# Induced attention and maxout MoE: the first part as one table of steps, its small diagonal products on GpSimd, and three high parts of the main loop made on VectorE

## The chip, the cores and the metric

One core of a Trainium2 chip runs one program. The metric is device microseconds of one execution, as the median of several. The kernel before takes 813.03 us.

## What is computed

```python
def mab(q, kv):                       # scale = 1/sqrt(128)
    a = softmax(scale * (q @ kv.transpose(0, 2, 1)))
    return a @ kv
h = mab(I, x)                         # I: 32 inducing rows, x: 4 x 12544 x 128
a = mab(x, h).reshape(50176, 128)
out = maximum(maximum(a @ w1, a @ w2), a @ w3) @ w_out      # 128 -> 768 -> 128
```

All data is float32. The kernel writes a float32 number as a high part of fewer bits (`hi`, cast to the type fp32r) and a low part (`lows`, the number less its high part) and multiplies the parts, so that TensorE's fast fp32r products keep the precision.

## The kernel before

The work has two stages. In the first stage the 12544 tokens of a batch lie in 7 groups, group 0 of 2 tiles and groups 1 to 6 of 16 tiles (of 128 tokens). For each group TensorE makes scores against the inducing rows (`attend_products`, line 353), VectorE takes the maximum (`mq`, line 391), a product with a small diagonal matrix `md` (line 398 makes it on ScalarE, line 405 multiplies) spreads the maxima over the partitions, VectorE reduces them (`mneg`, line 410), ScalarE takes the exponential (line 436), VectorE transposes (`aT`, line 465), and TensorE adds up the weighted tokens (line 489). The 7 partial results are combined to `hT` (line 663).

Batches 1 to 3 also come transposed from memory. Batch 0 doesn't: TensorE transposes its tiles (line 343), four to a bank, and ScalarE copies them out (line 345). So batch 0's first stage has nothing to hide behind and runs at the start of the program. Beside it the four weights come in as words of 64 bits and are converted on VectorE, in six steps each: `t` and `T` (lines 240, 244), `pw` (249), `rest` (253), an addition of `rest` and `t` (261, on GpSimd for three of the weights) and `dst` (265). `wcat` (269) is made of w1 and w3 less w2 on GpSimd, two instructions of 128x768.

The second stage has chunks of 512 tokens (the first chunk, of batch 0's group 0, has 256) and for each chunk 6 slots, one for each 128 of the 768 columns. A slot is a call of `advance` (line 813): TensorE makes `pu` and `pv` (820, 826), ScalarE a Relu of `pu` (835), VectorE their maximum `h` (853), ScalarE the high part `hi` (842), GpSimd, or VectorE for some of the slots, `lows` (850, 856). Six slots later TensorE multiplies both by `wo_hi` and `wo_lo` (lines 884 to 887). `h` needs a bank of which there are two, so TensorE waits for VectorE when `h` is late by more than one slot. 600 slots of this make up nearly all of the time, and the first part of the next batch runs inside them.

The scheduler is off: each engine works in the order in which the code issues its instructions. `phase1_first` (line 545) does batch 0's first stage in a loop over groups with the lists `LOADS` (the order of the DMA loads on SyncE's queue) and `WORK` (which steps of the weights stand behind which group), and the string `ORDER` sets the steps between `hT` and the main loop. Four buffers hold the 16-tile groups, and one more the sixth, so group 6's load waits until group 2 is used up.

## Time and profile before

| | |
|---|---|
| median of 3 runs (lowest, highest) | 813.03 us (812.34, 813.15) |
| span of the profiled execution | 811.8 us (its own time is not given apart; the median is 1.2 us above the span) |
| granted TensorE clock, mean | 1.000 |
| TensorE busy | 800.6 us (99%) |
| ScalarE busy | 734.8 us (91%) |
| GpSimd busy | 648.2 us (80%) |
| VectorE busy | 628.0 us (77%) |

The busy times are sums over the instructions of an engine. TensorE's part is 99% because 600 slots keep it filled; the eight-tenths of the first slice of the profile's forty are where it isn't.

### The profile page before, as it was taken

The page shows a single profiled execution, that of the slowest core. Times are in us where ns is not written, and L with a number is a line of the kernel's source. Part 1 is how long each engine was busy: PE and PEld are TensorE (multiplying, and loading weights), DVE is VectorE, ACT ScalarE, POOL GpSimd, SP SyncE. Part 2 cuts the span into 40 slices and gives each one's busy share as a digit, 9 for nine tenths or more (in the row PEclk, how much of TensorE's full clock was granted, in tenths as well). Part 3 has the DMA queues.
Part 4 walks back from the last instruction along what each step waited for, and adds up shares of the span by engine and source line. Part 5 has one row for each costly group of instructions (what it writes and reads, how often), then busy time and mean ns, then how long its engine had stood idle before and what let it go on. Part 6 is the DMA issues. An engine that isn't in the chain of part 4 may idle for free.

```text
span 811.8 us, 14334 instructions
## 1 busy us (share of the span) xinstructions
PE 800.6 (99%) x4561; PEld 629.4 (78%) x4561; DVE 628.0 (77%) x1067; ACT 734.8 (91%) x1532; POOL 648.2 (80%) x520
## 2 busy tenths in 40 slices
PE   8989999999999999999999999999999999999998
PEld 5758778777777787787877877878878788787887
DVE  4878878777877887877886878778778778778874
ACT  6779889899998998988998989889989999899996
POOL 1269879788788887886987978878879889788887
PEclk9999999999999999999999999999999999999999
DMA  8843234274542633533734426334223222222221
GB/s 327 318 141 111 75 122 145 85 244 157 178 134 69 192 116 103 192 117 108 233 113 123 118 99 197 112 105 134 69 77 102 66 72 78 66 87 73 62 79 52
DMA packets 52842, 102.51 MB, mean 126 GB/s; under 512 B 18208, under 2 KB 22176, under 8 KB 47520
## 3 DMA queue, kind: packets, MB, share of 16 engines
q1 hardware_dynamic: 52624, 101.47, 39.6%
q8 instruction: 36, 0.59, 0.3%
q14 instruction: 38, 0.31, 0.1%
q10 hardware_dynamic: 144, 0.13, 0.0%
HBM read 48.12 MB, written 25.69 MB: 91 GB/s over the span
## 4 chain that ended last, share of the span: by engine, by line
PE 96%; DMA 2%; SPq 1%; issue 0%; ACT 0%; DVE 0%; POOL 0%; POOLq 0%; ACTq 0%; DVEq 0%
PE acc L885 17%; PE pu L820 17%; PE pv L826 17%; PE acc L886 16%; PE acc L887 16%; PE aux L734 3%; PE acc L884 3%; PE acc L489 3%; PE aux L353 2%; DMA xg<-in_x_dram 2%; PE pu L343 0%; SPq L169 0%; PE pv L343 0%; POOL us L693 0%; PE aux L700 0%
## 5 line engine op out<-in xcount | busy, mean ns | idle before, releaser
L850 POOL TENSOR_TENSOR lows<-h,hi 128x512 fp32r<-128x512 f32 (+1 forms) x504 | 633.5, 1291 | 122.1 <-ACT hi L842 121.4
L853 DVE TENSOR_TENSOR h<-pv,ru 128x512 f32<-128x512 f32 (+1 forms) x600 | 403.4, 674 | 159.1 <-PE pv L826 99.8
L835 ACT ACTIVATE ru<-pu 128x512 f32<-128x512 f32 (+1 forms) x600 | 387.3, 645 | 51.3 <-PE pu L820 49.0
L842 ACT CAST hi<-h 128x512 fp32r<-128x512 f32 (+1 forms) x600 | 398.6, 664 | 0.3 <-DVE h L853 0.3
L820 PE MATMUL pu<-pT,us 128*128 128x512 f32 (+1 forms) x600 | 231.8, 387 | 1.8 <-ACT hi L842 0.9
L885 PE MATMUL acc<-hi,wo_hi 128*128 128x512 f32 (+1 forms) x594 | 231.8, 390 | 0.0
L826 PE MATMUL pv<-pT,us 128*128 128x512 f32 (+1 forms) x600 | 231.8, 386 | 0.1
L886 PE MATMUL acc<-hi,wo_lo 128*128 128x512 f32 (+1 forms) x594 | 228.9, 385 | 0.0
L887 PE MATMUL acc<-lows,wo_hi 128*128 128x512 f32 (+1 forms) x594 | 228.8, 385 | 0.0
L885 PEld LDWEIGHTS acc<-hi,wo_hi 128*128 128x128 f32 x594 | 111.5, 188 | 29.3 <-issue 7.5
L820 PEld LDWEIGHTS pu<-pT,us 128*128 128x128 f32 x600 | 112.5, 188 | 26.8 <-ACT ru L835 1.5
L826 PEld LDWEIGHTS pv<-pT,us 128*128 128x128 f32 x600 | 112.6, 188 | 23.7 <-DVE h L853 1.2
L887 PEld LDWEIGHTS acc<-lows,wo_hi 128*128 128x128 f32 x594 | 111.5, 188 | 22.7
L886 PEld LDWEIGHTS acc<-hi,wo_lo 128*128 128x128 f32 x594 | 111.6, 188 | 21.7
L856 DVE TENSOR_TENSOR lows<-h,hi 128x512 fp32r<-128x512 f32 x96 | 76.5, 797 | 0.8 <-ACT hi L842 0.8
L898 ACT COPY o<-acc 128x512 f32<-128x512 f32 (+1 forms) x96 | 61.6, 641 | 0.0
L884 PE MATMUL acc<-pT,us 128*128 128x512 f32 (+1 forms) x99 | 38.1, 385 | 0.0
L489 PEld LDWEIGHTS acc<-xg,aT 128*32 128x32 f32 x672 | 18.7, 110 | 9.4 <-issue 5.8
L353 PE MATMUL aux<-xT,iT 128*32 128x512 f32 x184 | 24.2, 597 | 1.7 <-ACT xT L345 1.7
L734 PE MATMUL aux<-xT,hT 128*32 128x512 f32 x192 | 25.1, 603 | 0.0
L261 POOL TENSOR_TENSOR rest<-rest,t 128x768 f32<-128x768 f32 x3 | 5.5, 1819 | 24.4 <-DVE rest L253 24.4
L489 PE MATMUL acc<-xg,aT 128*32 128x128 f32 x672 | 22.5, 273 | 0.0
(151 smaller groups left out, 446.2 us busy)
## 6 DMA issues: line engine op xcount, KB each, us to landing
out_dram<-o SPq DMA_DIRECT2D x95, 256.0 KB, 2.2
xg<-in_x_dram SPq DMA_DIRECT2D x23, 1024.0 KB, 5.9
xT<-in_xt_dram SPq DMA_DIRECT2D x18, 1024.0 KB, 5.3
pT<-ph SPq DMA_DIRECT2D x192, 64.0 KB, 2.0
pT<-pl SPq DMA_DIRECT2D x192, 64.0 KB, 2.0
raw<-in_w_dram SPq DMA_DIRECT2D x3, 768.0 KB, 8.5
us<-uh SPq DMA_DIRECT2D x24, 52.0 KB, 1.9
us<-ul SPq DMA_DIRECT2D x24, 52.0 KB, 2.6
```

The source lines that it names most:

```text
L489: nc.tensor.matmul(out=hps[q * M : (q + 1) * M, :], lhsT=aT[g][:, t * M : (t + 1) * M], rhs=xgs[g][:, t, :], start=(first[q] == k), stop=( ...
L820: nc.tensor.matmul(out=pu[:, :w], lhsT=state[c.b]["us"][:, 2 * j * P : (2 * j + 1) * P], rhs=c.pT[:, :w], start=True, stop=True)
L826: nc.tensor.matmul(out=pv[:, : d.w], lhsT=state[d.b]["us"][:, (2 * j + 1) * P : (2 * j + 2) * P], rhs=d.pT[:, : d.w], start=True, stop=True,)
L835: nc.scalar.activation(out=ru[:, :w], in_=pu[:, :w], func=AF.Relu)
L842: nc.scalar.copy(out=hi[:, : c.w], in_=h[:, : c.w])
L850: nc.gpsimd.tensor_sub(**args)
L853: nc.vector.tensor_max(out=h[:, : d.w], in0=pv[:, : d.w], in1=relus.pop(s)[:, : d.w])
L856: nc.vector.tensor_sub(**low)
L884: nc.tensor.matmul(out=to, lhsT=us[:, 2 * DF :], rhs=c.pT[:, cs], start=True, stop=False)
L885: nc.tensor.matmul(out=to, lhsT=wo_hi[:, j, :], rhs=c.hh[j][:, cs], start=False, stop=False)
L886: nc.tensor.matmul(out=to, lhsT=wo_lo[:, j, :], rhs=c.hh[j][:, cs], start=False, stop=False)
L887: nc.tensor.matmul(out=to, lhsT=wo_hi[:, j, :], rhs=c.hl[j][:, cs], start=False, stop=(j == NJ - 1))
```

## The change

The loop over groups is gone. One string has a step of one to five characters for each piece of work up to the main loop, and a function looks each up: `l` a load, `T` transposes and `C` the copy out of them (these were one call before), `S`, `M`, `D`, `P`, `L`, `E`, `V`, `U`, `K` the steps of a group, `w` with a number and a letter the steps of a weight (0 is w2, 1 w_out, 2 w1, 3 w3). The order on all engines is new. Beside it:

- `md` is made on GpSimd, for each of the 7 groups, and no longer on ScalarE.
- Group 6 has a buffer of its own, so its load waits for nobody.
- The low part of w_out (`wo_lo`) and the high part are steps of their own; `wo_lo` now follows the first `lows` on GpSimd.
- The high parts of the main slots 0, 6 and 8 are cast on VectorE.

```diff
-    LOADS = (0, 1, 2, 7, 3, 8, 4, 5, 9, 6, 10)
-    WORK = (
...
-    ORDER = "a a a a b a a b 0 c e m b a b a f b a p b 1 c s b b b s S m b q 2 c s 3 c s g s s s"
+    FIRST = (
+        "k0 l1 l0 k1 x1 T1.4 C1.4 x0 T1.8 li T0.0 is C0.0 l2 T1.12 C1.12 S0 l7 C1.8 T1.0 l3 M0 x2 next D0 "
...
+    )
...
+        elif (b, gi) == (0, NG - 1):
+            xg = xp.tile([P, GT, C], F32, name="xg6", tag="xg6", bufs=1)
...
-        nc.scalar.mul(out=md, in_=quad, mul=st["mq"])
...
+        nc.gpsimd.tensor_scalar(
+            out=st["md"][:, gi, :], in0=quad, scalar1=st["mq"].pop(gi), scalar2=None, op0=ALU.mult
+        )
...
+    HIVEC = (0, 6, 8)
...
-            nc.scalar.copy(out=hi[:, : c.w], in_=h[:, : c.w])
+            if s - 1 in HIVEC:
+                nc.vector.tensor_copy(out=hi[:, : c.w], in_=h[:, : c.w])
+            else:
+                nc.scalar.copy(out=hi[:, : c.w], in_=h[:, : c.w])
...
     with tc.manual_schedule(engines=MANUAL):
-        phase1_first()
...
+        for step in FIRST.split():
+            first(step, state[0])
```

How the order moves is shown at three places. In the rows a number behind a name (aux_79, acc_85, xg_131) only tells buffers apart.

SyncE's queue of loads, from the program's start, stood so before (`raw` of in_w_dram is w2, then w1, then w3):

```order
L548 DMA iT<-in_ind_t_dram 128x32
L169 DMA xgs<-in_x_dram 128x256
L169 DMA xg<-in_x_dram 128x512 x4
L169 DMA xg<-in_x_dram 128x2048
L189 DMA raw<-in_w_dram 128x1536
L169 DMA xg<-in_x_dram 128x2048
L189 DMA raw<-in_w_out_dram 128x6x256
L169 DMA xg<-in_x_dram 128x2048
L169 DMA xg_131<-in_x_dram 128x2048
L189 DMA raw<-in_w_dram 128x1536
L169 DMA xg<-in_x_dram 128x2048
L189 DMA raw<-in_w_dram 128x1536
```

The same queue now:

```order
L167 DMA xg<-in_x_dram 128x512 x4
L167 DMA xgs<-in_x_dram 128x256
L991 DMA iT<-in_ind_t_dram 128x32
L167 DMA xg<-in_x_dram 128x2048
L187 DMA raw<-in_w_dram 128x1536
L167 DMA xg<-in_x_dram 128x2048 x2
L187 DMA raw<-in_w_out_dram 128x6x256
L167 DMA xg_209<-in_x_dram 128x2048
L187 DMA raw<-in_w_dram 128x1536
L167 DMA xg_240<-in_x_dram 128x2048
L167 DMA xgs<-in_x_dram 128x256
L187 DMA raw<-in_w_dram 128x1536
```

Group 1's four pieces come first, group 4 is ahead of w_out, and group 6 (xg_240) follows w1 in a buffer that nothing else has used.

VectorE, from the transpose `aT` behind w1's `rest` to behind the minimum over all groups (`mmin`), where the `t` is w3's; before:

```order
L465 STREAM_TRANSPOSE aT<-a 128x512
L240 TENSOR_SCALAR t<-raw 128x768
L244 SCALAR_TENSOR_TENSOR t<-raw,t 128x768
L410 TENSOR_REDUCE mneg<-acc_85 128x1
L249 TENSOR_SCALAR pw<-t 128x768
L265 SCALAR_TENSOR_TENSOR dst<-size,rest 128x768
L391 TENSOR_REDUCE mq<-aux_79 128x1
L465 STREAM_TRANSPOSE aT<-a 128x512
L410 TENSOR_REDUCE mneg<-acc_85 128x1
L616 TENSOR_REDUCE mmin<-mneg 128x1
L253 SCALAR_TENSOR_TENSOR rest<-raw,pw 128x768
```

The same stretch of VectorE now:

```order
L465 STREAM_TRANSPOSE aT<-a 128x512
L237 TENSOR_SCALAR t<-raw 128x768
L465 STREAM_TRANSPOSE aT<-a 128x512
L389 TENSOR_REDUCE mq<-aux_80 128x1
L241 SCALAR_TENSOR_TENSOR t<-raw,t 128x768
L389 TENSOR_REDUCE mq<-aux_79 128x1
L410 TENSOR_REDUCE mneg<-acc_85 128x1
L262 SCALAR_TENSOR_TENSOR dst<-size,rest 128x768
L410 TENSOR_REDUCE mneg<-acc_85 128x1
L465 STREAM_TRANSPOSE aT<-a 128x512
L547 TENSOR_REDUCE mmin<-mneg 128x1
L246 TENSOR_SCALAR pw<-t 128x768
```

w3's `t` now stands ahead of two maxima `mq` (groups 5 and 6) instead of one, with one transpose between it and w1's `rest`; w3's `pw` went from ahead of w1's `dst` to behind `mmin`.

VectorE at the first main slots: before, from the `h` of slot 4 (128x256) to the first transpose of the next group's scores:

```order
L853 TENSOR_TENSOR h<-pv_83,ru 128x256
L853 TENSOR_TENSOR h<-pv_84,ru 128x256
L853 TENSOR_TENSOR h<-pv_83,ru 128x512
L853 TENSOR_TENSOR h<-pv_84,ru 128x512
L853 TENSOR_TENSOR h<-pv_83,ru 128x512
L853 TENSOR_TENSOR h<-pv_84,ru 128x512
L747 STREAM_TRANSPOSE aux_79<-aux_79 128x512
```

And the same stretch of VectorE now:

```order
L795 TENSOR_TENSOR h<-pv_83,ru 128x256
L795 TENSOR_TENSOR h<-pv_84,ru 128x256
L795 TENSOR_TENSOR h<-pv_83,ru 128x512
L782 CAST hi<-h 128x512
L795 TENSOR_TENSOR h<-pv_84,ru 128x512
L795 TENSOR_TENSOR h<-pv_83,ru 128x512
L782 CAST hi<-h 128x512
L795 TENSOR_TENSOR h<-pv_84,ru 128x512
L684 STREAM_TRANSPOSE aux_79<-aux_79 128x512
```

Two casts of 128x512 (slots 6 and 8) stand between the maxima, each ahead of the next `h`; the third, of slot 0, is 128x256 and stands ahead of these rows.

## Rows read from the trace of the kernel before

**Rows 1.** Busy time by stretches: stretch, then per engine (x instructions), clock, DMA share, GB/s

```profile
20.00:30.00 10.00, 8.83 (x123) 6.55 (x122) 8.69 (x13) 7.66 (x19) 1.96 (x2) 1.00 0.78 303
30.00:40.00 10.00, 9.35 (x150) 7.43 (x146) 8.74 (x18) 6.96 (x19) 3.49 (x2) 1.00 0.90 330
...
50.00:60.00 10.00, 8.74 (x55) 6.05 (x48) 7.58 (x15) 8.92 (x23) 7.42 (x9) 1.00 0.31 74
60.00:70.00 10.00, 10.00 (x46) 8.19 (x45) 9.55 (x18) 10.00 (x22) 10.00 (x9) 1.00 0.27 59
```

**Rows 2.** The page's chain that ended last, share of the span by engine

```profile
PE 96%; DMA 2%; SPq 1%; issue 0%; ACT 0%; DVE 0%; POOL 0%; POOLq 0%; ACTq 0%; DVEq 0%
```

**Rows 3.** TensorE's timeline: start, us, engine, line, operation [idle before <-releaser]

```profile
21.21 1.09 PE L343 MATMUL pu<-ident,xg 128*128 128x128 f32 x8 [1.17 <-DMA xg<-in_x_dram]
...
30.35 1.09 PE L343 MATMUL pu<-ident,xg 128*128 128x128 f32 x8
...
36.16 0.38 PE L405 MATMUL acc<-md,sel 128*128 128x4 f32 x2 [0.65 <-ACT md L398]
...
42.90 0.32 PE L734 MATMUL aux<-xTs,hT 128*32 128x64 f32 x8 [0.59 <-DVE hT L663]
...
55.94 0.28 PE L885 MATMUL acc<-hi,wo_hi 128*128 128x256 f32 x1
...
56.77 0.28 PE L885 MATMUL acc<-hi,wo_hi 128*128 128x256 f32 x1
...
61.50 0.40 PE L885 MATMUL acc<-hi,wo_hi 128*128 128x512 f32 x1
...
84.20 0.39 PE L887 MATMUL acc<-lows,wo_hi 128*128 128x512 f32 x1
```

**Rows 4.** VectorE's timeline, columns as in the timeline above

```profile
17.37 0.65 DVE L240 TENSOR_SCALAR t<-raw 128x768 uint32<-128x768 uint32 x1 [0.46 <-DMA raw<-in_w_out_dram]
...
20.59 0.69 DVE L391 TENSOR_REDUCE mq<-aux 128x1 f32<-128x512 f32 x1
21.19 0.70 DVE L465 STREAM_TRANSPOSE aT<-a 128x512 f32<-128x512 f32 x1
21.82 2.51 DVE L265 SCALAR_TENSOR_TENSOR wf<-size,rest 128x768 f32<-128x768 f32 x2
...
25.42 0.56 DVE L240 TENSOR_SCALAR t<-raw 128x768 uint32<-128x768 uint32 x1 [0.73 <-DMA raw<-in_w_dram]
...
85.27 3.63 DVE L856 TENSOR_TENSOR lows<-h,hi 128x512 fp32r<-128x512 f32 x1
...
89.42 0.68 DVE L856 TENSOR_TENSOR lows<-h,hi 128x512 fp32r<-128x512 f32 x1
```

**Rows 5.** GpSimd's timeline up to 92 us

```profile
15.78 1.82 POOL L261 TENSOR_TENSOR rest<-rest,t 128x768 f32<-128x768 f32 x1 [14.47 <-DVE rest L253]
...
17.66 0.50 POOL L501 MEMSET hg<- 64x128 f32 x1
...
20.82 1.82 POOL L261 TENSOR_TENSOR rest<-rest,t 128x768 f32<-128x768 f32 x1 [2.66 <-DVE rest L253]
...
35.26 1.81 POOL L269 TENSOR_TENSOR wcat<-dst,wf 128x768 f32<-128x768 f32 x1 [3.58 <-DVE dst L265]
...
56.41 1.53 POOL L850 TENSOR_TENSOR lows<-h,hi 128x256 fp32r<-128x256 f32 x2 [0.80 <-ACT hi L842]
...
58.21 30.14 POOL L850 TENSOR_TENSOR lows<-h,hi 128x512 fp32r<-128x512 f32 x24 [0.27 <-ACT hi L842]
```

**Rows 6.** Groups by line and shape: busy, mean ns of one, idle before

```profile
L265 DVE SCALAR_TENSOR_TENSOR dst<-size,rest 128x768 f32<-128x768 f32 x2 | 1.9, 954 | 0.0
...
L398 ACT ACTIVATE md<-quad,mq 128x4 f32<-128x4 f32 x7 | 2.1, 305 | 1.8 <-DVE mq L391 1.8
...
masks.py:197 POOL MEMSET ident<- 128x128 f32 x1 | 0.2, 204 | 0.3 <-POOLq L1124 0.3
...
L842 ACT CAST hi<-h 128x512 fp32r<-128x512 f32 x576 | 388.9, 675 | 0.3 <-DVE h L853 0.3
```

More of the change, by code (lines that the diff above doesn't have):

```diff
@@ L273, in convert, with transpose_w2, keep_w2 @@
             )
-    def work(steps):
-        for kind in steps.split():
-            convert(int(kind[0]), kind[1])
-    w2t = []
-    def transpose_w2():
-        for h in range(2):
-            tpw = bank_v[h]
-            for k in range(3):
-                j = 3 * h + k
-                nc.tensor.transpose(out=tpw[:, k * P : (k + 1) * P], in_=wf[:, 0, j * P : (j + 1) * P], identity=ident)
-            w2h = hp.tile([P, 512], F32, name="w2h", tag="ru", bufs=3)
-            nc.scalar.copy(out=w2h[:, : 3 * P], in_=tpw[:, : 3 * P])
-            w2t.extend(w2h[:, k * P : (k + 1) * P] for k in range(3))
+    w2t = {}
+    def transpose_w2(h):
+        tpw = bank_v[h]
+        for k in range(3):
+            j = 3 * h + k
+            nc.tensor.transpose(out=tpw[:, k * P : (k + 1) * P], in_=wf[:, 0, j * P : (j + 1) * P], identity=ident)
+    def keep_w2(h):
+        w2h = hp.tile([P, 512], F32, name="w2h", tag="ru", bufs=3)
+        nc.scalar.copy(out=w2h[:, : 3 * P], in_=bank_v[h][:, : 3 * P])
+        w2t.update((3 * h + k, w2h[:, k * P : (k + 1) * P]) for k in range(3))
     def prep_products():
@@ L323, in start_group @@
         st["xg"][gi] = xg_next.pop((b, gi))
-        ahead = max(NG, b * NG + gi + 4)
-        if ahead < B * NG:
-            key = (ahead // NG, ahead % NG)
-            if key not in xg_next:
-                xg_next[key] = load_group(*key)
         st["xT"][gi] = load_group_t(b, gi)
@@ new lines, in first @@
+    def first(step, st):
+        kind, rest = step[0], step[1:]
+        n = [int(k) for k in rest.split(".")] if rest.replace(".", "").isdigit() else []
+        two = {
+            "li": lambda: nc.sync.dma_start(out=iT, in_=ind_t),
+            "is": lambda: nc.scalar.mul(out=iT, in_=iT, mul=scale),
+            "cl": lambda: combine_least(st),
+            "cw": lambda: combine_weights(st),
+            "cm": lambda: combine_mask(st),
+            "sg": lambda: sum_groups(st),
+            "ts": lambda: total_sums(st, bank_o[0]),
+            "it": lambda: invert_total(st),
+            "cs": lambda: combine_states(st, NQ),
+            "o1": out_high,
+            "o2": out_low,
+            "next": lambda: start_batch(1),
+            "e0": lambda: attend_products(1, 0, bank_v[0]),
+            "e1": lambda: attend_products(1, 1, bank_v[1]),
+            "eg": lambda: attend_products(1, 2, bank_a[1]),
+            "ek": lambda: keep_scores(1),
+            "s": advance,
+            "a": lambda: next(steps["a"]),
+            "b": lambda: next(steps["b"]),
+            "k0": lambda: keep_busy(6, bank_o[1]),
+            "k1": lambda: keep_busy(2, bank_o[1]),
+            "k2": lambda: keep_busy(4, bank_o[1], P),
+            "G": prep_products,
+            "H": keep_products,
+        }
+        one = {
+            "l": first_load,
+            "n": lambda g: xg_next.__setitem__((1, g), load_group(1, g)),
+            "q": lambda g: load_channels(1, g),
+            "x": lambda g: start_group(0, g),
+            "T": lambda g, k: transpose_x(0, g, k),
+            "C": lambda g, k: keep_x(0, g, k),
+            "S": lambda g: attend_products(0, g, bank_a[g % 2]),
+            "M": lambda g: attend_max(0, g),
+            "D": lambda g: attend_column(0, g),
+            "P": lambda g, k: attend_spread(0, g, k, bank_o[0]),
+            "L": lambda g, k: attend_least(0, g, k),
+            "E": lambda g: attend_weights(0, g),
+            "V": lambda g: attend_transpose(0, g),
+            "U": lambda g: attend_sums(0, g, bank_o[1]),
+            "K": lambda g: attend_keep(0, g),
+            "y": transpose_w2,
+            "Y": keep_w2,
+            "c": lambda g: combine_groups(st, [g], bank_u[0]),
+            "s": lambda g: scores_products(0, g, bank_a[g % 2]),
+            "f": lambda k: first_products(st, k, bank_o[k % 2]),
+            "h": lambda k: first_high(st, k),
+            "z": lambda k: first_copy(st, k),
+            "v": lambda k: first_low(st, k),
+        }
+        if step == "pb":
+            chunks[0].pT = probs(chunks[0], bank_u[0])
+        elif step == "pq":
+            chunks[1].pT = probs(chunks[1])
+        elif kind == "w":
+            convert(int(rest[0]), rest[1])
+        elif step in two:
+            two[step]()
+        else:
+            one[kind](*n)
```

166 lines of the change are left out of this document (33 added, 133 removed), and 8 rows, old and new, of the table FIRST.

## The prediction

> **What bounds the kernel now.** I read the chain of waits first: 96% of it is TensorE [rows 2]. The table of stretches says where it isn't: from 60 us on TensorE is busy for all of every ten microseconds, but for 8.83, 9.35 and 8.74 of ten at 20, 30 and 50 us [rows 1]. After 60 us the change moves only the cast of an early slot, so it can win or lose only by shifting the point at which TensorE is full. I take as that point the first product with `hi` of the second chunk, at 61.50 [rows 3].
>
> Then I read what TensorE waits for ahead of it. Up to 21 us it is data: group 4's transposes begin at 21.21, behind 1.17 of waiting for its load [rows 3]. From there VectorE is nearly as full, 8.69 and 8.74 of ten [rows 1], and TensorE waits for the column `md` behind VectorE's maximum (0.65 at 36.16) and for `hT` (0.59 at 42.90) [rows 3]. So up to `hT` two things share the path, loads and VectorE, and a microsecond that VectorE loses there is one that `hT` comes later. Behind it is a ramp: six short slots take from 55.94 to 61.50, 5.56 us, where two neighbours stand 0.83 apart [rows 3], so 6 x 0.83 = 4.98 and 0.58 is lost.
>
> **The new order, a gain.** Group 6's load waited for the buffer of group 2, and its transposes began at 30.35 [rows 3]. Now it stands right behind w1 in the queue. Between group 4's arrival (21.2 [rows 3]) and w1's, for which VectorE's `t` waits until 25.42 [rows 4], came 1 MB and 0.75 MB, so 1 MB takes 2.4 us. w1 has the same bytes ahead of it as before; group 6 then lands at 25.4 + 2.4 = 27.8, and its transposes can start 2.5 us sooner. The bound on the other side: everything after that needs VectorE, which has the same work up to `hT` and was idle for only 1.3 us of each ten, so half of it, 1.2, may be all that comes through. I take 1.9, the middle, since neither row is nearer: **-1.9**. The other loads that moved (group 4 ahead of w_out, group 1 first) I cost at nothing, because TensorE waited there for group 4 and now has it before w_out; what this does to w_out is a rival below.
>
> **`md` on GpSimd.** Seven ScalarE instructions of 0.305 go [rows 6], which free nothing on the path, as ScalarE was idle for over two of ten there [rows 1]. No row shows so small a product on GpSimd. From below: a fill of 128x128 took 0.20 [rows 6], 0.1 less than ScalarE's. From above: it waits through one of VectorE's instructions with two inputs, 0.95 [rows 6], so 0.65 more. In GpSimd's queue the last two stand behind the addition for w1 (1.82), but so does w3's `t` on VectorE, ahead of their maxima, so GpSimd is free when they come. Only the last groups' is waited for (0.65 at 36.16 [rows 3]): between -0.1 and +0.65, **+0.3**.
>
> **Three casts leave ScalarE.** ScalarE is busy for 8.92 of ten in the ramp [rows 1], and gives up two casts of 0.675 [rows 6] and a smaller one. They can win no more than the ramp's loss of 0.58, and nothing if VectorE is what it waits for: **-0.5**, nearer the upper end because of the 8.92.
>
> **What falls together on VectorE and GpSimd, a loss.** Two instructions on VectorE (`dst` of w2 and w_out, two inputs each) took 2.51 from 21.82, where one takes 0.954 [rows 4, 6]: 0.6 too long. GpSimd ran 1.82 from 20.82 to 22.64 [rows 5], and 2.51 - 2 x 0.95 is just what VectorE would lose by waiting until about 0.14 before 22.64. The `t` of w_out at 17.37 took 0.65 and ended at 18.02 [rows 4], and GpSimd's fill of 64x128 that began at 17.66 took 0.50 [rows 5], though one of twice the size takes 0.20 [rows 6]; the two end together. So VectorE's instructions of one input (`t`, and by their kind `pw` and a cast) also seem to exclude GpSimd.
>
> In the new order such instructions stand beside GpSimd's 1.82 us in three places where they did not before. w1's `t` comes while GpSimd adds w_out's `rest` and `t`: between w_out's `rest` and it VectorE has a transpose and a maximum, 0.6 each from start to start (20.59, 21.19, 21.82 [rows 4]), so 1.82 - 0.14 - 1.2 is left, **+0.5**. w3's `t` follows w1's `rest` with only a transpose of 0.6 between; GpSimd starts its addition when `rest` is done, so about 1.82 - 0.14 - 0.6 = 1.1 is left, up to 1.3 where the transpose was ready at once: **+1.2**. w3's `pw` stood ahead of `dst`; now it comes after `dst`, two short minima and a transpose, while GpSimd makes `wcat` (1.81 from `dst` on [rows 5]); the three take 0.9 and wait a little for TensorE: 1.81 - 0.14 - 0.9 = 0.8 at most, **+0.5**. Each of the three may be 0, if GpSimd has finished, and the sum at most 3 x 1.68.
>
> **The casts on VectorE, a loss.** GpSimd's `lows` follow each other without a pause from 58.21, 24 in 30.14 us, 1.256 each [rows 5]. The casts of slots 6 and 8 come in the middle of this, each ahead of an `h` for which TensorE's banks wait. Slot 6 may come in the pause of 0.27 [rows 5]; slot 8 does not. From below 0; from above the row at 85.27, where VectorE's `lows` took 3.63 and not the 0.68 of 89.42 [rows 4], 2.95 lost. One `lows` less its last 0.14 is 1.1, and as most of such instructions do not look like 85.27 I take **+1.1**.
>
> Here the Trainium skill ("SBUF — State Buffer", section "Who interferes with whom") bears on the sum: `copy`, `cast` and `tensor_scalar` on VectorE in a two-port mode and GpSimd exclude each other for a whole instruction, whoever began first, and two SBUF inputs exclude a GpSimd instruction that reads. By that rule the cast loses one `lows` at most, so that the sum would stay at my 1.1; the row at 85.27 is more than two of them long, and goes against it.
>
> **`wo_lo`** moves from before the `lows` to behind the first of them, 1.81 of GpSimd. GpSimd stood idle for 0.80 + 0.27 in the ramp [rows 5], so its queue ends up 0.74 later. Its lead is thin: 26th `lows` done at 58.21 + 20 x 1.256 = 83.33, used at 84.20 [rows 3, 5], 0.87 ahead. 0.13 is left: I cost it at nothing, covered by this lead, and at up to 0.7 if the casts win all of the ramp's 0.58, as GpSimd is what is late next.
>
> **The sum:** -1.9 + 0.3 - 0.5 + 0.5 + 1.2 + 0.5 + 1.1 = +1.2. The profiled execution has a span of 811.8, and the median of 813.03 lies 1.2 above it, so a span of 813.0 and a time of **814.2**. A measurement of this kernel can tell about 0.2%, 1.6 us, from no change, so this is no change, on the slow side. Its own range goes from 812.8 (order 2.5, the rest as it is) to 815.4 (order 1.2, `md` 0.65).
>
> **Rivals.** (1) *The engines don't meet.* If `t`, `pw` and the casts don't exclude GpSimd (the evidence is one 0.65 and one 0.50), or come when it rests, only the order's gain is left: -1.9 + 0.3 - 0.5 = -2.1, 810.9. For it: each meeting depends on times of a few tenths that I shifted myself. Against: three instructions and two casts would all have to miss. (2) *VectorE starves*, the case on the slower side. The cast of slot 8 waits through one `lows` and, because GpSimd's next one is ready, through another, as at 85.27. It decides at the point where `wo_lo` has built a queue on GpSimd: with a `lows` waiting, GpSimd goes on. Then the cast costs up to 2.95 in place of 1.1: +3.0, 816.0. For it: GpSimd has no pause from 58.21 on. Against: only one such row stands out. (3) *w_out is late.* With group 4 ahead of it, w_out comes at about group 4's old time, 21.2 in place of 17.3, and its `t` stands ahead of group 3's maximum on VectorE. If that maximum waits, the order gives 0.9 and not 1.9: +2.2, 815.2.
>
> **How the numbers follow.** My forecast has 0.49, rival 1 0.24, rival 2 0.17, rival 3 0.10. Faster by over 0.2% (under 811.4): nearly all of rival 1, 0.21. Slower by over 0.2% (over 814.65): rival 2, most of 3, and a quarter of the forecast, 0.36. Within: 0.43. The range from 810.9 to 816.3 leaves out a little less than half of rival 1 and of rival 2, together just under 0.2.
>
> **What would show it.** Group 6's transposes near 28 and not 30.35. w3's `t` near 30 at 1.6 to 1.9 us and not 0.56, w1's `t` and w3's `pw` at about 1.0; if they have 0.56, rival 1 is right. The casts on VectorE: slot 8's at about 1.5 (forecast), 0.4 (rival 1), 2.7 or more (rival 2). TensorE's start on `hT` about 0.6 later than 42.90, the second chunk's first `hi` product at about 62.7 and not 61.50. TensorE full after that in both; a wait for `lows` near 83 would show that the lead was too thin, and I would be wrong there.

## The result, and the profile after

The changed kernel takes 817.05 us (median of 4 runs, 816.43 to 817.84), the kernel before 813.09 beside it. The ratio is 1.0051, with a 95% interval from 1.0037 to 1.0065, so it is slower by about 4 us, where 1.2 was forecast and the range ended at 816.3. The profiled execution, the slowest of the four, has a span of 816.1 us, 4.3 more than that of before.

The timelines of the two show where the 4.3 come from. I read five points in each: the start of VectorE's `hT`, TensorE's first `pu` of 512 columns, the second chunk's first product with `hi`, the 27th product with `hi` (counted from the first chunk's first), and the end.

| us | before | after | longer by |
|---|---|---|---|
| start to `hT` | 42.55 | 44.19 | +1.64 |
| `hT` to the first 512-wide `pu` | 12.39 | 13.47 | +1.08 |
| from there to the second chunk's first `hi` | 6.56 | 7.06 | +0.50 |
| from there to the 27th `hi` | 27.28 | 28.34 | +1.06 |
| from there to the end | 723.02 | 722.99 | 0 |

All of it lies ahead of 95 us. TensorE's timeline in the profile of after has these rows (start, us, engine, line, operation, idle before and its releaser):

```profile
10.85 0.63 PE L336 MATMUL pv<-ident,xg 128*128 128x128 f32 x4 [1.31 <-DMA xg<-in_x_dram]
...
28.37 1.06 PE L336 MATMUL pu<-ident,xg 128*128 128x128 f32 x8
...
34.49 0.38 PE L405 MATMUL acc<-md,sel 128*128 128x4 f32 x2 [1.46 <-POOL md L396]
...
36.32 0.39 PE L405 MATMUL acc<-md,sel 128*128 128x4 f32 x2 [0.42 <-POOL md L396]
36.56 2.64 PE L290 MATMUL pu<-wf,w2h 128*128 128x128 f32 x12
39.13 1.61 PE L489 MATMUL acc<-xg,aT 128*32 128x128 f32 x32
...
57.66 0.47 PE L759 MATMUL pu<-pT,us 128*128 128x512 f32 x1 [1.56 <-DMA pT<-pl]
...
62.95 0.50 PE L765 MATMUL pv<-pT,us 128*128 128x512 f32 x1 [0.23 <-DVE h L795]
...
84.97 0.47 PE L759 MATMUL pu<-pT,us 128*128 128x512 f32 x1 [0.78 <-DMA pT<-pl]
```

Group 6's transposes begin at 28.37 and no longer at 30.35 [rows 3]: the load came early, as it should. But TensorE then waits 1.46 and 0.42 for `md`, and the next products take 2.64 for twelve and 1.61 for thirty-two, where before's trace has 1.58 and 1.08 for the same groups. TensorE's rows of before for these, and for the first `pu` of 512 columns:

```profile
36.41 1.58 PE L296 MATMUL pu<-wf,w2h 128*128 128x128 f32 x12
37.92 1.08 PE L489 MATMUL acc<-xg,aT 128*32 128x128 f32 x32
...
54.94 0.47 PE L820 MATMUL pu<-pT,us 128*128 128x512 f32 x1 [0.87 <-ACT hi L842]
```

The table of stretches of after shows why; its columns are the stretch, its length, the busy time of the five engines, the granted clock, the DMA share and GB/s:

```profile
30.00:40.00 10.00, 8.12 (x117) 5.87 (x119) 9.06 (x15) 5.55 (x13) 5.51 (x4) 0.84 0.26 103
...
33.00:36.50 3.50, 1.62 (x40) 1.29 (x36) 2.90 (x5) 1.58 (x4) 2.17 (x3) 1.00 0.06 21
36.50:41.00 4.50, 4.24 (x46) 3.67 (x46) 4.23 (x10) 1.15 (x4) 1.55 (x1) 0.62 0.01 4
```

TensorE was busy for 1.62 of 3.50 us, and was then granted 0.62 of its clock on the average of 4.50, that is 1.2 GHz for most of it and 2.4 after. In the kernel before this stretch had 1.00 [rows 1]. The two groups of products lost 1.06 + 0.53 = 1.6 us.

The other two waits that are new, 1.56 and 0.78, are for copies: SyncE moves the probabilities `ph` and `pl` into `pT` in small DMAs, one after another. Here is SyncE's queue in the kernel after:

```profile
53.56 2.51 SPq L740 DMA_DIRECT2D pT<-pl  x2
...
81.03 2.40 SPq L740 DMA_DIRECT2D pT<-pl  x2
```

The same two pairs in the kernel before, at 52.18 and 77.82, and two pairs that are slow there:

```profile
52.18 1.17 SPq L803 DMA_DIRECT2D pT<-pl  x2
...
56.17 1.90 SPq L803 DMA_DIRECT2D pT<-ph  x2
...
77.82 1.14 SPq L803 DMA_DIRECT2D pT<-pl  x2
...
81.22 1.95 SPq L803 DMA_DIRECT2D pT<-pl  x2
```

What else moved on the DMA engines from 53.56 to 56.07 in the kernel after is in the DMA view of that stretch (queue, packets, MB, share of 16 engines):

```profile
q8 instruction: 1, 0.02, 3.9%
```

A packet of this queue carries instructions. The page has 36 of them in either kernel, 0.59 MB in all, so 16 KB each. Here one of them ran beside the copies of `pl`. That this is no chance I read in all seventeen traces, pair by pair between 45 and 88 us: 26 pairs of `ph` or `pl`, or trains of six `mx`, are slow (1.60 us or more where the other pairs take at most 1.56, or 4.21 or more and not 3.7), and beside each of the 26 runs such a packet. Not every copy beside a packet is slow. The kernel before has two slow pairs itself, but TensorE waits for neither.

VectorE's timeline answers to the collisions that were forecast [rows 4]; the first two rows are the `t` of w_out and group 3's maximum:

```profile
19.91 0.56 DVE L237 TENSOR_SCALAR t<-raw 128x768 uint32<-128x768 uint32 x1
...
21.80 0.69 DVE L389 TENSOR_REDUCE mq<-aux 128x1 f32<-128x512 f32 x1 [0.34 <-PE aux L351]
...
25.82 0.60 DVE L237 TENSOR_SCALAR t<-raw 128x768 uint32<-128x768 uint32 x1 [0.44 <-DMA raw<-in_w_dram]
...
30.52 1.69 DVE L237 TENSOR_SCALAR t<-raw 128x768 uint32<-128x768 uint32 x1
...
37.48 0.98 DVE L246 TENSOR_SCALAR pw<-t 128x768 uint32<-128x768 uint32 x1
...
59.65 0.50 DVE L782 CAST hi<-h 128x512 fp32r<-128x512 f32 x1
...
61.45 0.84 DVE L782 CAST hi<-h 128x512 fp32r<-128x512 f32 x1
```

w3's `t` (30.52) took 1.69 and `pw` 0.98, as forecast; w1's `t` took 0.60 because it waited for its data until GpSimd had nearly finished. The casts took 0.50 and 0.84. And `md`, by the groups by line and shape (busy, mean ns), is dearer than its 305 ns on ScalarE [rows 6]:

```profile
L396 POOL TENSOR_SCALAR md<-quad,mq 128x4 f32<-128x4 f32 x7 | 5.0, 714 | 17.4 <-DVE mq L389 16.6 <-DVE mneg L410 0.8
```

### The profile page after: what moved, and what is told of

Its sections match the earlier page's. It is cut to its first block, busy times and chain, and to the rows that moved or that the text cites. A ratio compares the mean times of both kernels' runs of the same rounds, so it can differ in the third digit from the quotient of the medians.

```text
span 816.1 us, 14339 instructions
## 1 busy us (share of the span) xinstructions
PE 801.8 (98%) x4561; PEld 630.1 (77%) x4561; DVE 628.7 (77%) x1070; ACT 732.8 (90%) x1522; POOL 652.5 (80%) x527
## 4 chain that ended last, share of the span: by engine, by line
PE 93%; DMA 3%; DVE 1%; ACT 1%; SPq 0%; issue 0%; POOL 0%; DVEq 0%; ACTq 0%
PE acc L827 17%; PE pv L765 16%; PE pu L759 16%; PE acc L828 16%; PE acc L829 16%; PE aux L671 3%; PE acc L826 3%; PE acc L489 2%; PE aux L351 2%; DMA raw<-in_w_dram 2%; DMA xg<-in_x_dram 1%; DMA pT<-pl 1%; PE pu L290 0%; SPq L167 0%; PE aux L637 0%
## 5 line engine op out<-in xcount | busy, mean ns | idle before, releaser
L784 ACT CAST hi<-h 128x512 fp32r<-128x512 f32 (+1 forms) x597 | 394.3, 660 | 1.0 <-DVE h L795 0.7
L826 PEld LDWEIGHTS acc<-pT,us 128*128 128x128 f32 x99 | 18.6, 188 | 3.7
```

Source lines behind the costliest of these rows:

```text
L784: nc.scalar.copy(out=hi[:, : c.w], in_=h[:, : c.w])
L826: nc.tensor.matmul(out=to, lhsT=us[:, 2 * DF :], rhs=c.pT[:, cs], start=True, stop=False)
```

## The experiments

Theory after the result: the order is a gain, and it is lost three times over: to the half clock behind idle, to instruction packets beside small copies, and to the casts. The rivals were that single parts (`md`, the casts) bear the loss, or that the order gains nothing. Each run's points are in one table (us; the last column but one counts executions whose mean granted clock was 0.998 or less). The kernel before, run beside them, has such a low clock in 13 of 130 executions.

| run | to `hT` | to `pu` | to `hi` | to 27th | median | before | ratio, 95% interval | low clock | profile's end |
|---|---|---|---|---|---|---|---|---|---|
| e1_casts_act | 41.64 | 13.16 | 6.57 | 28.30 | 815.30 | 813.01 | 1.0023 (1.0008, 1.0037) | 6 of 10 | 812.65 |
| e2_md_act | 41.70 | 12.13 | 7.70 | 28.36 | 815.74 | 813.01 | 1.0033 (1.0020, 1.0046) | 5 of 10 | 812.88 |
| e3_clock | 43.46 | 12.66 | 7.24 | 28.09 | 815.41 | 813.01 | 1.0034 (1.0022, 1.0045) | 2 of 10 | 814.56 |
| e4_fetch | 43.74 | 12.65 | 7.23 | 27.83 | 815.18 | 813.01 | 1.0024 (1.0011, 1.0036) | 2 of 9 | 814.52 |
| e5_after_again | 41.86 | 12.86 | 7.08 | 28.47 | 815.91 | 812.81 | 1.0030 (1.0018, 1.0043) | 4 of 9 | 813.24 |
| e6_filled_act | 42.90 | 12.90 | 6.57 | 27.80 | 814.91 | 812.81 | 1.0022 (1.0011, 1.0033) | 1 of 10 | 813.17 |
| e7_before_casts | 43.12 | 12.38 | 7.08 | 27.31 | 813.48 | 812.81 | 1.0004 (0.9993, 1.0014) | 0 of 10 | 812.98 |
| e8_before_md | 45.47 | 12.38 | 6.56 | 27.25 | 817.01 | 812.81 | 1.0054 (1.0032, 1.0076) | 5 of 5 | 814.71 |
| e9_t_late | 42.37 | 12.93 | 7.08 | 28.36 | 814.47 | 813.40 | 1.0015 (1.0003, 1.0027) | 4 of 10 | 813.77 |
| e10_aligned | 43.56 | 12.14 | 6.57 | 27.73 | 814.67 | 813.40 | 1.0019 (1.0009, 1.0029) | 1 of 10 | 813.77 |
| e11_before_shift | 42.79 | 13.09 | 6.56 | 27.59 | 814.55 | 813.40 | 1.0015 (1.0006, 1.0024) | 0 of 10 | 813.05 |
| e12_best | 41.94 | 12.13 | 6.56 | 27.72 | 813.54 | 812.49 | 1.0013 (1.0004, 1.0022) | 0 of 11 | 812.20 |
| e13_no_fill | 40.94 | 13.09 | 6.58 | 28.29 | 814.02 | 812.49 | 1.0020 (1.0011, 1.0029) | 5 of 11 | 811.95 |
| e14_shift_more | 43.65 | 12.14 | 6.56 | 27.24 | 814.58 | 812.78 | 1.0014 (1.0005, 1.0023) | 0 of 11 | 812.81 |
| e15_shift_in_wait | 41.64 | 12.14 | 6.57 | 27.25 | 812.35 | 812.75 | 0.9991 (0.9982, 1.0000) | 0 of 11 | 810.57 |

From the 27th `hi` to the end all take 722.97 to 723.22, but for e10_aligned and e12_best with 723.77 and 723.85.

### The parts by themselves

**e1_casts_act** gives the casts back to ScalarE, **e2_md_act** gives `md` back.

```diff
-    HIVEC = (0, 6, 8)
+    HIVEC = ()
```

> The changed kernel with all high parts back on ScalarE. Theory (the casts on VectorE cost the ramp): slot 8's cast took 0.84 and slot 6's 0.50 on VectorE and TensorE then waited 0.23 and 0.3 for the maxima behind them, so the stretch from the first 512-wide pu product (57.66) to the second chunk's first hi product (64.72) falls from 7.06 to about 6.6 as before, 0.5 us less in all. Rival (ScalarE bounds the ramp, the casts on VectorE help): that stretch grows by up to 0.5. Second rival (GpSimd's lows are the bound by 84 us): the ramp gets shorter but a wait for lows near 84 takes it back, 0 in all. The wait of 1.56 for the low part's copy at 57.66 stays in all of these.

```diff
-        nc.gpsimd.tensor_scalar(
-            out=st["md"][:, gi, :], in0=quad, scalar1=st["mq"].pop(gi), scalar2=None, op0=ALU.mult
-        )
+        nc.scalar.mul(out=st["md"][:, gi, :], in_=quad, mul=st["mq"].pop(gi))
```

> The changed kernel with the seven md products back on ScalarE. Theory (md on GpSimd costs because it waits for VectorE's instructions, 0.30 alone but 0.93 and 1.00 for groups 5 and 6): TensorE's waits of 1.46 and 0.42 for md shrink by about 0.7 each, and the shorter idle stretch keeps TensorE's clock at full speed, so the 3.4 us at half clock from 36.9 are gone too: hT 1.2 to 2.8 earlier, 1.2 to 2.8 us less in all. Rival (my prediction's price, 0.3 for md, the idle time being VectorE's order): hT 0.3 earlier, clock still half from 36.9. If only the clock is the effect: hT about 1.7 earlier with md's wait nearly as before.

With the casts back the ramp is 6.57, that of before (6.56): so the three together cost 0.5, what they take less what ScalarE's relief gives. With `md` back on ScalarE `hT` comes at 41.70, with it on GpSimd at 41.64, and group 2's transposes begin at 10.05 and 10.06: `md` has no price on the path where the clock holds. Nor does the low clock need it in the new order: five of ten executions have it with `md` on ScalarE.

Both profiles have the full clock and an `hT` 0.9 earlier than before's profile, so the 44.19 of after was no property of the order alone. They do not show a gain of the order, though, because before's profiled execution was longer than most. In every execution of these runs the time is 1.73 to 1.92 above the span, so its span of 811.8 stands for 813.5 at least, and the executions of before at a clock over 0.998 have medians of 812.5 to 812.9. What lies behind `hT` is the same within 0.1 in the profiles of e8_before_md and, less its casts, of e7_before_casts, so the usual `hT` of before is at about 41.7. The medians of e1_casts_act, e2_md_act and e5_after_again put theirs, by the same way, at 41.5 to 41.9. These are estimates from times, spans and the table; by them the order with its collisions gains nothing ahead of `hT`.

In e2_md_act the last cast met a `lows` in full, in VectorE's timeline, and the ramp became 7.70:

```profile
57.60 1.51 DVE L780 CAST hi<-h 128x512 fp32r<-128x512 f32 x1
```

**e5_after_again** is the changed kernel itself, once more and with more executions.

> The changed kernel as it is, executed again, to see how its time goes with TensorE's mean granted clock. Theory (a stretch or two of 3.4 us at half clock costs about 1.7 us each, and TensorE's idle stretch decides): most executions show a mean clock of 0.996 to 0.998, those at 0.999 or 1.000 take 814.5 to 815.5, those below 816 to 818. Rival (the clock has no part in it): the times of both kinds lie together within 0.5 us, near 817.

Its profile has the full clock, behind nearly the same two waits:

```profile
10.26 0.63 PE L336 MATMUL pv<-ident,xg 128*128 128x128 f32 x4 [0.72 <-DMA xg<-in_x_dram]
...
33.77 0.39 PE L405 MATMUL acc<-md,sel 128*128 128x4 f32 x2 [1.40 <-POOL md L396]
...
35.59 0.38 PE L405 MATMUL acc<-md,sel 128*128 128x4 f32 x2 [0.43 <-POOL md L396]
35.83 1.58 PE L290 MATMUL pu<-wf,w2h 128*128 128x128 f32 x12
```

The five executions with a clock of 0.999 or more took 814.95 to 815.91, the four with 0.997 took 816.26 to 817.42. All four of the first measurement had 0.997 or 0.998. So the same kernel meets the half clock in some executions and not in others, for about 2 us (medians 815.06 and 817.03), and that was half of the loss first measured; at the full clock 2.4 are left. From group 2's transposes to `hT` it takes 31.60 here and 33.34 in after's profile, so of the 2.33 between the two `hT` the half clock has 1.74, and 0.59 is group 2's load, which came later there (10.85 and not 10.26).

**e7_before_casts** and **e8_before_md** make one part of the change in the kernel before.

```diff
-            nc.scalar.copy(out=hi[:, : c.w], in_=h[:, : c.w])
+            (nc.vector.tensor_copy if s - 1 in (0, 6, 8) else nc.scalar.copy)(out=hi[:, : c.w], in_=h[:, : c.w])
```

> The kernel before with the casts of slots 0, 6 and 8 alone moved to VectorE. Theory (a cast there waits for a lows of GpSimd and TensorE for the maximum behind it): the stretch from the first 512-wide product (54.94) to the second chunk's first hi product (61.50) grows from 6.56 by 0.5 to 1.1, and the time by the same, 813.5 to 814.1 us. Rival (they relieve ScalarE): that stretch falls by up to 0.5, 812.5 us. Clock 1.000 in all.

```diff
-        nc.scalar.mul(out=md, in_=quad, mul=st["mq"])
+        nc.gpsimd.tensor_scalar(out=md, in0=quad, scalar1=st["mq"], scalar2=None, op0=ALU.mult)
```

> The kernel before with the seven md products alone moved to GpSimd. Theory (0.3 us of its own, up to 0.95 where VectorE runs an instruction with two inputs or a fast one beside it): md takes 0.3 to 1.0; hT moves by 0.0 to +0.7, clock 1.000, 813.0 to 813.7 us. Rival (md is what cost most in the changed kernel): hT 1.3 later or more, over 814.3 us, or a stretch at half clock.

The casts cost 0.5 in the ramp here too (7.08 and not 6.56). `md` costs far more in the old order than in the new: `hT` comes 2.9 later than in before's profile, with group 4's transposes at 21.08 and not later than before's 21.21. The last `md` stands behind `wcat` on GpSimd, TensorE waits 1.88, and then runs at half its clock for most of 39 to 43 us, where the table of stretches has 0.57 (thirty-two products took 1.08 elsewhere in this trace):

```profile
37.52 0.39 PE L405 MATMUL acc<-md,sel 128*128 128x4 f32 x2 [1.88 <-POOL md L398]
...
39.34 1.94 PE L489 MATMUL acc<-xg,aT 128*32 128x128 f32 x32
41.21 2.19 PE L637 MATMUL pu<-sw,hg 128*128 128x64 f32 x12
```

```profile
39.00:43.00 4.00, 4.00 (x46) 3.34 (x45) 3.12 (x7) 0.83 (x4) 0.73 (x1) 0.57 0.62 201
```

**e9_t_late** moves w3's `t` on VectorE behind group 5's maximum, past GpSimd's addition.

```diff
-        "... C6.0 C6.12 S5 w3t V4 ... U3 M5 K3 w3T D5 ..."
+        "... C6.0 C6.12 S5 V4 ... U3 M5 K3 w3t w3T D5 ..."
```

> The changed kernel with w3's t put behind group 5's maximum on VectorE, so that it no longer meets GpSimd's addition for w1. Theory (meeting that addition costs 1.1 on the way to hT): t takes 0.56 and not 1.69 to 1.86, group 5's maximum begins when its scores are there, about 31.3 and not 32.8 in the full-clock run's times, hT 0.8 to 1.1 earlier than 41.9 at full clock, and TensorE's wait of 1.4 for md shrinks by as much, so fewer executions fall to half clock. Rival (what bounds hT there is the sum of VectorE's work, not the meeting): hT within 0.3 of 41.9. The loss behind hT stays.

```profile
32.80 0.56 DVE L237 TENSOR_SCALAR t<-raw 128x768 uint32<-128x768 uint32 x1
```

It takes 0.56, and its executions at full clock 813.46 to 814.53, against 814.95 to 815.91 in e5_after_again. Set against the kernel before of the same runs, the medians at full clock are 1.5 and 2.4 above: the collision was worth about 0.9, and lay on the path. Its profile fell to half the clock in another place, behind a wait of 1.43 for group 2's load. In the table of stretches:

```profile
11.60:15.10 3.50, 3.50 (x17) 1.92 (x10) 1.69 (x3) 1.42 (x4) 0.53 (x1) 0.51 1.01 428
```

### The clock

Filler products on constants, whose results are unused, keep TensorE busy where it waits: **e3_clock** ahead of the wait for `md`, **e4_fetch** ahead of group 2's transposes, **e6_filled_act** in both places with the casts on ScalarE.

```diff
-        "U3 M5 K3 w3T D5 S6 P5.5 ..."
+        "U3 M5 K3 w3T D5 S6 k3 P5.5 ..."
...
+            "k3": lambda: keep_busy(8, bank_o[1], P),
```

> The changed kernel with eight more products of zeros and ones on TensorE, 128x384, in its wait from 33.0 to 34.5, results unused. Theory (TensorE's clock fell to half from 36.9 to 40.3 because TensorE had stood idle for most of 33 to 36.5): the clock stays at 1.00, the twelve products of w2 and w_out take 1.58 and not 2.64 and the sums of group 5 1.08 and not 1.61, hT is about 1.4 us earlier. Rival (the fall has another cause, or the path to hT is VectorE's): the clock falls all the same, or hT moves by less than 0.3. Sixteen more instructions on TensorE also move the 16 KB instruction packet that ran at 54.1: by the theory on that packet it comes earlier, and the wait of 1.56 for the copy shrinks or goes.

```diff
-        "P0.0 L0.0 T2.8 l4 ..."
+        "P0.0 L0.0 k3 T2.8 l4 ..."
```

> The changed kernel with eight more products of 128x384 on TensorE in its wait for data at 9.5 to 10.85, results unused. Theory (the copy of the low part for the second chunk landed at 57.5 and not 55.9 because a 16 KB instruction packet of TensorE, one for each 256 of its instructions, ran at 54.13 to 55.70 on one of the DMA engines): sixteen more instructions bring that packet to about 52 to 53, where the copies have only begun, so the wait of 1.56 falls to 0.3 to 0.6, about 1 us less; the packet at 80.9 also moves, and the wait of 0.78 at 84.97 falls. Rival (the copy is late because the load of 1 MB issued at 46.19 runs until 53.1): the wait stays at 1.5. The clock still falls at 36.9 in both.

> The changed kernel with all high parts on ScalarE and eight more products of 128x384 on TensorE in each of two waits (for data at 9.5 to 10.85, for md at 33.0 to 34.5), results unused. Theory (the three losses are the clock, the instruction packets beside the copies of the probabilities, and the casts): clock 1.000 in nearly all executions; the packets move by 32 instructions, so the waits for copies at 57.7 and 85.0 go; hT about 0.9 earlier than before the change, 12.4 from it to the first 512-wide product, 6.6 from there to the second chunk's hi product, about 27.3 from there to the 27th hi slot; 811.5 to 812.5 us, faster than the kernel before by 0.5 to 1.5. Rival (the new order itself is slower by the exclusions of VectorE and GpSimd, as I predicted): hT 0.6 later than before, 813.5 to 814.5 us.

Filling one place leaves a clock of 0.998 in two of ten and two of nine executions, filling both in one of ten, filling none in four to six of nine to eleven. The counts of the runs with one place filled are too few to tell the two apart; that the clock can fall behind either idle, e9_t_late's and after's profiles show, one each, and in e4_fetch's profile, with the wait for `md` left as it was (1.39), it fell there again. But none of the three gave what was expected (e6_filled_act 814.91, for 811.5 to 812.5). In their profiles `hT` is at 42.90 to 43.74, later than in e5_after_again's at full clock. In e6_filled_act that is the load: group 2's transposes began at 11.30, behind the fillers and 0.92 of waiting for the data, and from there to `hT` it took 31.60, as in e5_after_again, so the filled wait for `md` cost nothing. e3_clock is no clean test: there w3's square on ScalarE came after 3.30 of idle, which the profile puts down to GpSimd's `md` and which the changed kernel does not have.

```profile
36.47 0.93 ACT L256 ACTIVATE size<-raw 128x768 f32<-128x768 f32 x1 [3.30 <-POOL md L396]
```

### The packets of instructions

e4_fetch was also a first test of the packets: sixteen more instructions of TensorE ahead of them. The way from `hT` to `pu` fell from after's 13.47 to 12.65 and that to the 27th `hi` from 28.34 to 27.83, with 0.73 of waiting left at that `pu`, against the rival that the load of 1 MB delays the copy. **e10_aligned** is e6_filled_act with the fillers as 256-wide products, twice as many of them at the start and twelve in each of the two waits, so that packets come at other times; **e11_before_shift** adds fillers to the kernel before for the same end.

```diff
-            "k0": lambda: keep_busy(6, bank_o[1]),
-            "k1": lambda: keep_busy(2, bank_o[1]),
+            "k0": lambda: keep_busy(12, bank_o[1], 2 * P),
+            "k1": lambda: keep_busy(4, bank_o[1], 2 * P),
...
+            "k3": lambda: keep_busy(12, bank_o[1], 2 * P),
```

> The changed kernel with all high parts on ScalarE, and its first filling products cut in two (16 of 256 for 8 of 512 columns) and twelve products of 256 columns in each of the two waits: 32 TensorE products more than the changed kernel, 16 more than the run with eight in each wait. Theory (a 16 KB instruction packet costs 0.3 to 1.2 us when it runs beside the train of small copies, 11 to 19 us behind the second chunk's first hi product): the packet that ran at 75.1 runs about 3 us earlier, ahead of the train, the wait at 82 is 0 and the stretch to the 27th hi slot is 27.3 as before the change; clock 1.000; 812 to 813 us at full clock. Rival (that stretch is longer for another reason): it stays at 27.8 or more.

```diff
+            if gi < 3:
+                keep_busy(3, bank_o[1], 3 * P)
...
+                keep_busy(8, bank_o[1], 3 * P)
```

> The kernel before with 17 more products of 128x128 of ones and zeros on TensorE, in waits it has anyway (three each ahead of three groups' scores, eight in the wait for group 4's load), results unused. Theory (the packets' place decides): the fifth 16 KB packet, at 81.6 or 20.1 behind the second chunk's first hi product, comes 3 to 4 us earlier, into the train of copies, and TensorE then waits 0.5 to 1.0 near 82, the stretch to the 27th hi slot grows from 27.28 to 27.9 to 28.5; hT stays within 0.5 of 42.6; 0.5 to 1.2 us slower than the kernel before. Rival (the new order, not the packet, makes the copies late): that stretch stays at 27.3.

In e10_aligned the way from `hT` to `pu` falls to 12.14, so 1.3 of after's 13.47 were the packet's; against before's 12.39 the new order is 0.25 shorter here without it. e11_before_shift is no clean counterpart: its copies of `mx` at 73.62 took 4.21 and not 3.72 beside a packet, as meant, but its 13.09 come from a load of `xT` that took 6.3 to landing and not 4.6, with no packet beside it. Its 814.55 show only that the kernel before loses over a microsecond too when its products are shifted. At the slots ahead of the 27th `hi` e10_aligned still lost 0.45, in small parts: the products with `hi` there follow each other in 1.15 to 1.26 and not 1.13, which is the 1.256 that GpSimd needs for a `lows` [rows 5]. `wo_lo` had used up its lead.

**e12_best** puts together what the runs pointed at (casts on ScalarE, `t` late, `wo_lo` ahead of the `lows`, fillers with `k0` and `k1` as in e10_aligned), **e13_no_fill** is the same without new fillers.

```diff
-        "... L0.0 T2.8 ... T6.8 w2A C6.0 C6.12 S5 w3t V4 ... U3 M5 K3 w3T D5 ... U4 q1 D6 L5.5 P6.6 ... w3S a e1 ... s s o2 v2 ..."
+        "... L0.0 k3 T2.8 ... T6.8 w2A C6.0 C6.12 S5 V4 ... U3 M5 K3 w3t w3T D5 ... U4 q1 D6 L5.5 k4 P6.6 ... w3S o2 a e1 ... s s v2 ..."
...
+            "k2": lambda: keep_busy(6, bank_o[1], 2 * P),
+            "k3": lambda: keep_busy(14, bank_o[1], 2 * P),
+            "k4": lambda: keep_busy(8, bank_o[1], 2 * P),
```

> The changed kernel with everything that the runs pointed at: the three casts back on ScalarE, w3's t behind group 5's maximum (as in e9_t_late), wo_lo made straight after w3's dst and so ahead of all lows, and 256-wide filler products (results unused) in place of the 128-wide ones, with more of them so that the 16 KB packets of instructions fall off the copies of ph and pl. Theory (order worth 0.7 to 0.9 and more with t late, packets 1.0 to 1.3 in hT to pu6, 0.8 to 1.0 in slots 19 to 23, clock at full): hT at 41.5 or before, hT to the first 512-wide pu 12.1 to 12.4, the second chunk's ramp 6.6, its first hi to the 27th 27.3, span end 810.5 to 811.5, time 811.5 to 812.8 where the kernel before has 813.1. With wo_lo ahead, GpSimd's lead over its first use at slots 19 to 23 is 1.8 us larger than in e10_aligned, so no spacing over 1.13 there. Rival (the order's gain is always lost again in the main loop, because GpSimd and VectorE limit it and not TensorE): first hi to 27th stays at 27.7 or more and the time at 813.5 to 814.7 like e9_t_late and e10_aligned.

> The same as e12_best without any change of the filler products: only casts back on ScalarE, w3's t late, wo_lo ahead of the lows. Theory: the packets fall as in e1_casts_act, so hT to the first 512-wide pu 12.6 to 13.4 and one spacing of 2 us at slots 19 to 23, which costs 0.8 to 1.0 against e12_best there, and half of the executions meet the half clock: time 813.3 to 814.5, 1 to 2 above e12_best. Rival (it was GpSimd's lead and not the packet at slots 19 to 23): with wo_lo ahead the spacings there are 1.13 without fillers too, and e13_no_fill is within 0.5 of e12_best.

e13_no_fill has the earliest `hT` of all, 40.94, 1.6 ahead of that in before's profile (0.4 to 0.6 ahead by the estimate from the medians), and loses it again: 1.0 on the way to `pu`, and 1.0 at one slot, where SyncE and TensorE read

```profile
76.89 2.39 SPq L740 DMA_DIRECT2D pT<-pl  x2
```

```profile
80.84 0.47 PE L759 MATMUL pu<-pT,us 128*128 128x512 f32 x1 [0.78 <-DMA pT<-pl]
```

GpSimd had its lead back in this run, so this place is the packet's alone. The rival in its expectation falls by the spacing of 2.15 there, although the median is within 0.5 of e12_best's, as the rival had it: e12_best lost as much elsewhere. In e12_best both places are clear, but other packets fell on other copies: six of `mx` took longer, and at the very end ScalarE's last copy waited for the output. SyncE's and ScalarE's rows:

```profile
71.80 4.36 SPq L417 DMA_DIRECT2D mx<-mx  x6
```

```profile
809.04 0.37 ACT L840 COPY o<-aux 128x256 f32<-128x256 f32 x1 [4.10 <-DMA out_dram<-o]
```

A packet of q8 runs beside each of the two (from 72.28 and from 805.84). e12_best missed its 811.5 to 812.8 by that, and by group 2's load, which TensorE got at 11.74 and not at 10.26 as in e13_no_fill; why that execution's load was late stays open.

**e14_shift_more** and **e15_shift_in_wait** are e12_best with 8 more small products ahead of these packets, in e14_shift_more at the start, in e15_shift_in_wait in the wait for `pn` behind `hT`.

```diff
-            "k0": lambda: keep_busy(12, bank_o[1], 2 * P),
-            "k1": lambda: keep_busy(4, bank_o[1], 2 * P),
+            "k0": lambda: (keep_busy(8, bank_o[1], 2 * P), keep_busy(8, bank_o[1], 3 * P)),
+            "k1": lambda: keep_busy(8, bank_o[1], 3 * P),
```

> e12_best with 8 more filler products of the same total columns in the first 5 us (results unused), where TensorE waits for loads anyway, so that every later packet of instructions comes 8 products earlier: the one that delayed the six copies of mx from 71.80 (4.36 us and not 3.72) falls ahead of them, the one beside the last full out copy (4.0 us to landing and not 2.0) ahead of that. Theory (packets decide): mx x6 3.7, spacing of slots 22 and 23 1.13 (e12_best: 1.57 and 1.39), first hi to 27th 27.3, from the 27th hi to the end 723.0 (e12_best: 723.85): 1.2 to 1.5 less than e12_best, 812.0 to 812.4, at or under the kernel before. Rival (the lost time in slots 22 and 23 and at the end is not the packets'): within 0.4 of e12_best, 813.1 to 813.9.

```diff
-        "... h0 v0 b pb s2 b z1 ..."
+        "... h0 v0 b k5 pb s2 b z1 ..."
...
+            "k5": lambda: keep_busy(8, bank_u[0], 3 * P),
```

> e12_best with its 16 filler products at the start as they were (24 of them took 5.38 us in e14_shift_more and 16 took 3.78, so those 8 put the whole first part off by 1.6), and the 8 more placed ahead of the transpose of pn, where TensorE waited 0.96 for VectorE. Theory (packets decide, and the order gains 0.6 to 1.6 at hT): hT as in e12_best, 41.2 to 41.9, hT to the first 512-wide pu 12.1 to 12.3, mx x6 3.7, first hi to 27th 27.3, 27th hi to the end 723.0 to 723.2, time 811.2 to 812.3, faster than the kernel before by 0.5 to 1.2. Rival (something else in the order takes the gain back): 812.5 or more.

e14_shift_more had the packets clear (27.24, and 723.22 to the end) and lost it at the start: its own fillers there took 5.38 and not 3.78, in TensorE's timeline, and `hT` came 1.7 later than in e12_best.

```profile
1.61 5.38 PE L543 MATMUL acc<-ident_r 128*128 128x256 f32 x24 [1.61 <-DVE ident_r L201]
```

e15_shift_in_wait has both: 812.35, just above the 811.2 to 812.3 it was given, with the clock at 1.000 in all eleven executions. Its ratio to the kernel before is 0.9991 where e12_best has 1.0013, and the two kernels differ by 8 more products in a wait and nothing else. In the profiles 0.47 of this lies ahead of the 27th `hi` and 0.88 behind it; another 0.30 lies ahead of `hT`, where e12_best's load was late. Its rows for the copies of `mx` and for the last copy:

```profile
71.53 3.72 SPq L417 DMA_DIRECT2D mx<-mx  x6
```

```profile
807.40 0.37 ACT L840 COPY o<-aux 128x256 f32<-128x256 f32 x1 [3.29 <-PE aux L829]
```

It is the fastest version here, where the changed kernel had ratios of 1.0051 and 1.0030; the 0.4 us to the kernel before are at the edge of what can be told (0.9982 to 1.0000).

## Why the prediction was wrong

- **Forecast: no change, slower side; result: slower by 4.0.** The direction of the lean was right, the size not: +1.2 was the sum, and two costs had no term in it, the half clock (1.6) and the packets (1.3 and 1.1). All four executions first measured had the low clock; with the full clock the changed kernel is slower by 2.4 (e5_after_again).
- **The step that failed first: "`md` on GpSimd ... +0.3".** I priced a wait of TensorE as that wait and no more, here and in the whole sum, which has no term for the clock. As a wait the term was at most too high (`hT` is the same within 0.1 with and without `md` on GpSimd, e1_casts_act and e2_md_act). But TensorE was busy for only 1.62 of 3.50 us around the two waits for `md`, and the granted clock fell, for 1.6 us. `md` is not the only way to it: with `md` on ScalarE five of ten executions have the low clock, and e9_t_late's profile has it behind the wait for group 2's load (0.51). In the old order `md` alone does it, in five of five executions (e8_before_md). With the idle places filled, e12_best, e14_shift_more and e15_shift_in_wait have the low clock in none of 33, and e13_no_fill, without the fillers, in five of eleven.
- **The second: "after 60 us the change moves only the cast of an early slot".** It also moved when the packets of instructions come. One beside the copies of `pl` ahead of the ramp cost 1.3 (12.13 in e2_md_act, 12.14 in e10_aligned, 13.47 after), one at the third chunk 1.0 to 1.1 (27.25 in e15_shift_in_wait, 28.29 in e13_no_fill, 28.34 after). Before's had happened to fall on copies that TensorE doesn't wait for. I had read the waits of TensorE, but not what shares the DMA engines with a copy that nothing delays yet.
- **The order, "-1.9", stays open between two readings.** `hT` was forecast 0.6 later, collisions included. In the profiles at full clock it came 0.7 to 0.9 earlier, and with the extra times of w3's `t` (about 0.9), of w1's `t` in e5_after_again and of `pw` (0.4 each) the order alone would give about 2.4. By the medians, which allow for the long execution in before's profile, `hT` is where it was, within 0.3, and the order alone would give about 1.4 to 2.0. Both are estimates, and of the three extra times only that of w3's `t` is shown to lie on the path.
- **The collisions were right as times.** w3's `t` 1.69 (forecast 1.6 to 1.9), `pw` 0.98 (1.0); w1's `t` missed GpSimd in after's profile (0.60) and met it in e5_after_again's (0.98). e9_t_late shows that w3's is worth about 0.9 of the 1.2 that it was charged with, against rival 1. The rule of the Trainium skill ("SBUF — State Buffer", section "Who interferes with whom") holds for all of these: none waited for more than one of GpSimd's instructions, the longest waits being those of w3's `t` (1.69 here and 1.86 in e5_after_again, where 0.56 is usual, beside an instruction of 1.84) and of the cast of 1.51.
- **The casts: "+1.1" and "-0.5" were right in their sum, +0.6 for a measured 0.5.** The terms by themselves were not run apart. The casts took 0.50 and 0.84, where the forecast had about 1.5 for the second. Rivals 1 and 2 did not come. Nor did rival 3 (w_out late): the `t` of w_out ran at 19.91 without a wait for its data, and group 3's maximum behind it waited for TensorE.
- **`wo_lo`: "a wait for lows near 83 would show that the lead was too thin".** After's profile has no such wait, because the wait for `pl` stands there; with it gone e10_aligned lost 0.45, and with `wo_lo` ahead e15_shift_in_wait lost nothing there, which fits a lead that was too thin.
- **In the sums:** the lower end of the range is not 812.8 but 814.2 - 0.6 = 813.6. The time was put 1.2 above the span, by a median and a span of different executions, where every execution that has both shows 1.73 to 1.92; with that the forecast would have been about 814.7. And by the row at 21.82 the wait on GpSimd ended 0.22 ahead of 22.64, not 0.14.
- **Open:** why the same wait is followed by the half clock in one execution and not in the next, and what delays the first loads in some.
